# Eight PSUM banks shared out anew in a fused attention and mixer kernel: from 2 + 2 + 4 to 3 + 2 + 3

## The chip, the cores and the metric

The kernel runs on one core of one Trainium2 chip. The metric is the time of one execution on the device in microseconds (us), and the figure that counts is the median of several runs.

## What is computed

The inputs are q, k and v (8 batches, 8 heads, 576 tokens, 64 numbers per head) and seven weight matrices. Cut to what matters:

```python
k_p = k.reshape(B, H, 72, 8, D).mean(axis=3)      # keys and values pooled by eights
v_p = v.reshape(B, H, 72, 8, D).mean(axis=3)
attn = softmax(q @ k_p.T / sqrt(D)) @ v_p          # x: (8, 576, 512)
theta = x @ w_theta
y = w_tok_r @ (x * cos(theta)) + w_tok_i @ (x * sin(theta))
u = x + y
x = u + relu(u @ w_ch)
h = relu(x.T @ w_tok1) @ w_tok2                    # over tokens
u = x + h.T
out = u + relu(u @ w_ch1) @ w_ch2
```

## The kernel before

The work runs in three stretches. The **attention stage** goes up to about 545 us of the span: a prologue computes attention for batch 0 and converts the weights, and then a loop over the eight batches does the token products of batch b while it computes, in between, the attention, the angles and the factors of batch b + 1. After it come the channel product and the token mixer (to about 775 us) and the large channel mixer (to the end).

Every matrix product and every transpose writes into one of eight PSUM banks of 512 numbers per partition. A bank is taken by name. Three kinds of names exist, and each kind is handed out in rotation by its own counter (line 129):

- **m** (line 137): the token products. `mix_part` (line 770) takes one for each group of 27 matrix products (line 786). The bank is free again when VectorE has added it to the tile R (line 789).
- **t** (line 140): theta, in `emit_theta` (line 676). Free when ScalarE has read it (line 705) and VectorE has subtracted it (line 718).
- **x** (line 143): all the rest of the attention stage. `emit_sc` (line 538) takes two for each pair of heads, for scores of chunks 0 to 1 and 2 to 4; VectorE frees them by a maximum and a subtraction (lines 552 and 553). `emit_pt` (line 579) takes two for each transpose of the softmax; ScalarE copies them (604, 608) and VectorE takes the rest (605, 610). `emit_av` (line 616) takes one for each product with the values; ScalarE copies it twice (645, 646) and VectorE frees it (650). `emit_z` (line 725) takes one for the transposes of R; VectorE frees it (736, 745). In batch 0 the copies are those of lines 601 and 631. `pool_k`, `pool_v` and `pool_vl` take some x banks in the prologue.

```python
    def bank(kind, n):
        i = bank_i.get(kind, 0)
        bank_i[kind] = i + 1
        nm = f"{kind}{i % n}"
        need(nm)
```

The token products of a batch are eight groups of 27. `interleave` (line 793) puts the steps of the next batch's attention between them at moments that the table `P` (line 20) lists. The program is then put in its final order by a scheduler, engine by engine, which goes by its own estimate of when a bank or a tile is free. So the order of the instructions is fixed before the kernel runs, and an engine that comes to an instruction whose bank is still in use waits there, with all that stands behind it in its queue. The softmax of a pair of heads runs over three engines: subtract on VectorE (553), exponent on ScalarE (558), sum and reciprocal on VectorE (564, 565, 568), scaling on GpSimd (569, 574). The tile R gets a copy of its tail by line 536 before theta of the last token chunk can begin.

In the two later stretches all eight banks are taken in one fixed rotation by `bank_any` (line 148).

Of the kernel before, what the change touches and what calls it, by code (L numbers as in the profile page):

```python
# [64 lines left out]
def tile_attn_moe(  # L65
# [43 lines left out]
    def need(*tags):  # L109
        while any(t in d[3] for d in dq for t in tags):  # L110
            run_one()
# [17 lines left out]
# [5 lines that stand above are left out]
        last_bank[0] = nm  # L134
        return pp.tile([128, 512], F32, tag=nm, name=nm)

    def bank_m():
        return bank("m", 2)

    def bank_t():  # L140
        return bank("t", 2)

    def bank_x():
        return bank("x", 4)

    allseq = [0]

    def bank_any():
        i = allseq[0] % 8
        allseq[0] += 1  # L150
        nm = ("m0", "t0", "x0", "x1", "m1", "t1", "x2", "x3")[i]
        need(nm)
        return pp.tile([128, 512], F32, tag=nm, name=nm)

# [316 lines left out]
    def pool_k(b, g):  # L471
        t, m = kn_t[b], pool_t[0]
        ps = bank_x()
        for i in range(2):
            ds = slice((2 * g + i) * 128, (2 * g + i + 1) * 128)
            o = ps[:, i * 80:i * 80 + 80]
            for c in range(4):
                mm(o[:, 8 + 16 * c:24 + 16 * c], t[:, c, ds], m[:, 0:16], True, True)
            for c0 in (0, 72):
                mm(o[:, c0:c0 + 8], t[0:64, 4, ds], m[0:64, 0:8], True, True)  # L480
        v = ps[:, 0:160].rearrange("p (g k) -> p g k", g=2)
        nc.vector.tensor_copy(out=bdk[0:64, 2 * g:2 * g + 2, 0:72], in_=v[0:64, :, 0:72])
        nc.scalar.copy(out=bdk[64:128, 2 * g:2 * g + 2, 72:144], in_=v[64:128, :, 8:80])

    def pool_v(b):
        t, m = vn_t[b], pool_t[0]
        ps = bank_x()
        for c in range(4):
            mm(ps, m[:, 64 - 16 * c:192 - 16 * c], t[:, c], c == 0, c == 3)
        v = ps.rearrange("p (j e d) -> p j e d", j=4, e=2)  # L490
        for e in range(2):
            pr = slice(64 * e, 64 * e + 64)
            if b == 0:
                (nc.vector.tensor_copy, nc.scalar.copy)[e](out=vb0[pr, :, pr], in_=v[pr, :, e])
            else:
                nc.scalar.copy(out=vbh[pr, :, pr], in_=v[pr, :, e])
        if b > 0:
            def fin():
                for e in range(2):
                    pr = slice(64 * e, 64 * e + 64)  # L500
                    nc.vector.tensor_sub(
                        out=vlo["b"][pr, :, pr], in0=v[pr, :, e], in1=vbh[pr, :, pr].bitcast(F32)
                    )

            later(1.0, fin, last_bank[0], "vbl")

    def pool_vl(b):
        t, m = vn_t[b], pool_t[0]
        ps = bank_x()
        mm(ps, m[0:64, 192:320], t[0:64, 4], True, True)  # L510
        v = ps.rearrange("p (h d) -> p h d", h=8)

        def masked(o, pr):
            nc.vector.tensor_tensor(
                out=o[pr].rearrange("p a e d -> p (a e) d"), in0=v[pr],
                in1=mask[pr].unsqueeze(2).to_broadcast([64, 8, 64]), op=ALU.mult,
            )

        lo, up = slice(0, 64), slice(64, 128)
        if b == 0:  # L520
            masked(vl0, lo)
            return
        tm = st("kr", [128, 4, 2, 64], F32, "vlt")
        vll = vlo["l"]
        masked(tm, lo)
        masked(vlh, up)
        nc.scalar.copy(out=vlh[lo], in_=tm[lo])
        nc.gpsimd.tensor_sub(out=vll[lo], in0=tm[lo], in1=vlh[lo].bitcast(F32))
# [241 lines left out]
    def mix_part(b, half, jj, th, part, hold):  # L770
        j = 2 * half + jj
        t0, n = TH[th]
        ts = slice(t0, t0 + n)
        if part == 0:
            hold["ps"] = bank_m()
        o = hold["ps"][:, 0:n]
        need(f"Z{half}", f"zt{b % 2}")
        z, zt = z_t[b, half], zt_t[b]
        for i in range(part * 3, part * 3 + 3):
            (a, w), s = HL3[i // 9], i % 9  # L780
            cq_upto(9 + s + 9 * th)
            if s < 8:
                lhsT = z[:, a, s // 4, s % 4, jj * 128:(jj + 1) * 128]
            else:
                lhsT = zt[:, a, j * 128:(j + 1) * 128]
            mm(o, lhsT, wtk[s][:, w, ts], i == 0, i == 26)
        if part == 8:
            R = r_t[b]
            nc.vector.tensor_add(out=R[:, j, ts], in0=o, in1=R[:, j, ts])  # L789
            if th == 1:  # L790
                nc.sync.dma_start(out=scr_u[b][:, j, :], in_=R[:, j, 0:T])
# [75 lines left out]
    def emit_ch(b, j, th):  # L867
        t0, n = TH[th]
        ts = slice(t0, t0 + n)
        h = uh_t[b]  # L870
        o = bank_any()[:, 0:n]
        i = 0
        for a, w in HL3:
            for k in range(4):
                mm(o, wch[k][:, w, j * 128:(j + 1) * 128], h[a][:, k, ts], i == 0, i == 11)
                i += 1
        u = u_t[b][:, j, ts]
        nc.vector.scalar_tensor_tensor(out=u, in0=o, scalar=0.0, in1=u, op0=ALU.max, op1=ALU.add)
        gate[0] = u[0:1, 0:1]
        if j == 3 and th == 1:  # L880
            dup_tail(u_t[b], nc.scalar.copy)

    def emit_tr(b, c):
        u = u_t[b]
        if c == 0:
            x2_t[b] = (st("Z0", [128, 2, 4, 512], F32R, "x2"), st("zt0", [128, 512], F32R, "x2t"))
        x2, x2t = x2_t[b]
        ps = bank_any()
        for d in range(4):
            src = u[:, d, c * 128:(c + 1) * 128]  # L890
            tp(ps[:, d * 128:(d + 1) * 128], src)
        if c < 4:
            nc.scalar.copy(out=x2[:, 0, c, :], in_=ps)
            nc.vector.tensor_sub(out=x2[:, 1, c, :], in0=ps, in1=x2[:, 0, c, :].bitcast(F32))
        else:
            nc.scalar.copy(out=x2t, in_=ps)
            lo = x2t[64:128]
            nc.vector.tensor_sub(out=lo, in0=ps[64:128], in1=lo.bitcast(F32))

    def emit_tok1(b, f):  # L900
        x2, x2t = x2_t[b]
        w1 = A2["tok1"]
        if f == 0:
            h1_t[b] = (st("tmp0", [128, 2, 512], F32R, "h1a"), st("tmp1", [128, 2, 512], F32R, "h1b"))
        fs = slice(f * 128, (f + 1) * 128)
        ps = bank_any()
        seq = [(w1[:, w, s, fs], x2[:, a, s, :]) for a, w in HL3 for s in range(4)]
        seq += [(w1[:, 0, 4, fs], x2t), (w1[:, 1, 4, fs], x2t)]
        for i, (l, r) in enumerate(seq):
            mm(ps, l, r, i == 0, i == len(seq) - 1)  # L910
        h = h1_t[b][f]
        nc.scalar.activation(out=h[:, 0], in_=ps, func=ACTF.Relu)
        nc.vector.scalar_tensor_tensor(
            out=h[:, 1], in0=ps, scalar=0.0, in1=h[:, 0].bitcast(F32), op0=ALU.max, op1=ALU.subtract
        )
# [726 lines left out]
```

## Time and profile before

| | |
|---|---|
| Median of 3 runs | 1333.22 us (1333.06 to 1338.38) |
| The profiled execution | 1337.11 us |
| Its span, first to last instruction | 1335.3 us |
| TensorE busy with matrix products | 1277.9 us, 96% of the span |
| VectorE busy | 976.6 us, 73% |
| ScalarE busy | 637.1 us, 48% |
| GpSimd busy | 315.5 us, 24% |
| Granted TensorE clock, mean | 0.993 of full speed |

PE stands for TensorE, PEld for its weight loads, DVE for VectorE, ACT for ScalarE, POOL for GpSimd. In the timeline views a row gives the start, the time to the end of the last of the merged instructions, the engine and line, what is written from what (buffer numbers left out), and how many instructions are merged; in square brackets stands the idle time of the engine just before, and what ended it.

### The profile page before, as it was taken

The page shows a single profiled execution, that of the slowest core. Times are in us where ns is not written, and L with a number is a line of the kernel's source. Part 1 is how long each engine was busy: PE and PEld are TensorE (multiplying, and loading weights), DVE is VectorE, ACT ScalarE, POOL GpSimd, SP SyncE. Part 2 cuts the span into 40 slices and gives each one's busy share as a digit, 9 for nine tenths or more (in the row PEclk, how much of TensorE's full clock was granted, in tenths as well). Part 3 has the DMA queues.
Part 4 walks back from the last instruction along what each step waited for, and adds up shares of the span by engine and source line. Part 5 has one row for each costly group of instructions (what it writes and reads, how often), then busy time and mean ns, then how long its engine had stood idle before and what let it go on. Part 6 is the DMA issues. An engine that isn't in the chain of part 4 may idle for free.

```text
span 1335.3 us, 22342 instructions
## 1 busy us (share of the span) xinstructions
PE 1277.9 (96%) x8214; PEld 1216.5 (91%) x8216; DVE 976.6 (73%) x1749; ACT 637.1 (48%) x1190; POOL 315.5 (24%) x340
## 2 busy tenths in 40 slices
PE   6899999999999999999999999999999999999998
PEld 4588999999999998998889988888999999999998
DVE  7987667584958696566676768688665489987893
ACT  4765454555564564233333246466454354444442
POOL 4553324232433533111110001111100013133112
PEclk9999999999999999999999999999999999999999
DMA  9423122221322023445567367767544986556521
GB/s 330 145 81 118 58 97 81 85 91 60 108 64 69 28 89 115 145 162 211 196 237 261 128 206 256 237 202 244 202 155 166 335 318 216 163 187 208 185 94 69
DMA packets 119613, 213.70 MB, mean 160 GB/s; under 512 B 11152, under 2 KB 65936, under 8 KB 119504
## 3 DMA queue, kind: packets, MB, share of 16 engines
q1 hardware_dynamic: 119504, 212.29, 46.9%
q8 instruction: 64, 1.05, 0.3%
q14 instruction: 45, 0.37, 0.1%
HBM read 133.60 MB, written 78.64 MB: 159 GB/s over the span
## 4 chain that ended last, share of the span: by engine, by line
PE 55%; DVE 21%; issue 11%; DMA 8%; POOL 2%; ACT 2%; SPq 0%; DVEq 0%; POOLq 0%; ACTq 0%
PE x L159 20%; PE m L159 18%; PE t L159 15%; DMA scr_g<-g 2%; DVE sm L564 2%; PE x L173 2%; DVE e L553 2%; DVE mx L552 2%; DMA raw_n<-scr_x 1%; DVE tmp L736 1%; DMA scr_w<-wo 1%; DVE sm L565 1%; POOL wo L1024 1%; DMA ws<-w_ch 1%; DVE R L789 1%
## 5 line engine op out<-in xcount | busy, mean ns | idle before, releaser
L159 PE MATMUL m<-wtk,Z 128*128 128x256 f32 (+1 forms) x1536 | 247.1, 300 | 7.4 <-DVE R L789 7.1
L159 PEld LDWEIGHTS m<-wtk,Z 128*128 128x128 f32 x1536 | 218.0, 190 | 10.7 <-DVE R L789 7.7
L751 POOL TENSOR_TENSOR Z<-tmp,Z 128x1024 fp32r<-128x1024 f32 x31 | 74.7, 2411 | 110.9 <-ACT Z L750 110.9
L1012 POOL TENSOR_TENSOR wsum<-wm 128x128 f32<-128x128 f32 (+1 forms) x18 | 10.8, 602 | 298.8 <-DVE wm L1002 281.7
L159 PE MATMUL t<-wth,Xh 128*128 128x256 f32 (+1 forms) x504 | 76.5, 293 | 0.5 <-DVE Xh L536 0.2
L1364 POOL TENSOR_TENSOR o<-o,u 128x384 f32<-128x384 f32 x12 | 16.2, 1374 | 244.5 <-DVE u L1352 156.3
L159 PEld LDWEIGHTS t<-wth,Xh 128*128 128x128 f32 x504 | 67.0, 188 | 4.5 <-DVE Xh L536 1.8
L718 DVE SCALAR_TENSOR_TENSOR tmp<-tmp,t 128x512 f32<-128x512 f32 x40 | 27.3, 684 | 53.9 <-ACT tmp L705 53.9
L159 PE MATMUL x<-ope_Xl,wa 128*128 128x384 f32 x336 | 65.4, 336 | 0.1
L159 PE MATMUL m<-ope_Z,wa 128*128 128x384 f32 x300 | 63.7, 337 | 1.3 <-ACT p L1264 0.6
L159 PE MATMUL x<-ope_R,wa 128*128 128x384 f32 x312 | 62.4, 340 | 0.7 <-DVE p L1281 0.7
L736 DVE TENSOR_TENSOR tmp<-x,tmp 128x1024 f32<-128x1024 f32 x32 | 39.1, 1221 | 31.1 <-ACT tmp L712 16.0
L159 PE MATMUL x<-ope_Z,wa 128*128 128x384 f32 x276 | 56.1, 339 | 4.4 <-ACT p L1277 2.5
L159 PEld LDWEIGHTS x<-ope_Xl,wa 128*128 128x128 f32 x336 | 58.8, 188 | 0.4 <-DVE ope_Xl L1126 0.4
L159 PE MATMUL x<-bdk,q 128*128 128x144 f32 x320 | 47.9, 303 | 11.5 <-DVE bdk L1423 7.0
L159 PEld LDWEIGHTS x<-ope_R,wa 128*128 128x128 f32 x312 | 54.6, 188 | 2.6 <-DVE p L1281 1.8
L159 PEld LDWEIGHTS x<-bdk,q 128*128 128x128 f32 x320 | 44.4, 203 | 13.6 <-issue 10.8
L159 PE MATMUL m<-wtk,zt 128*128 128x256 f32 (+1 forms) x192 | 56.8, 296 | 0.0
L159 PE MATMUL x<-ope_Xh,wa 128*128 128x384 f32 x264 | 54.9, 340 | 1.9 <-DVE p L1281 0.8
L159 PEld LDWEIGHTS m<-ope_Z,wa 128*128 128x128 f32 x300 | 52.9, 188 | 2.2 <-ACT p L1264 0.9
L159 PEld LDWEIGHTS x<-ope_Z,wa 128*128 128x128 f32 x276 | 48.2, 188 | 6.7 <-ACT p L1277 3.5
L705 ACT ACTIVATE tmp<-t,magic 128x512 f32<-128x512 f32 x40 | 27.3, 684 | 55.6 <-PE t L159 42.8
(412 smaller groups left out, 3521.6 us busy)
## 6 DMA issues: line engine op xcount, KB each, us to landing
wa<-scr_w SPq DMA_DIRECT2D x42, 512.0 KB, 5.5
scr_g<-g SPq DMA_DIRECT2D x108, 192.0 KB, 2.4
scr_w<-wo SPq DMA_DIRECT2D x42, 256.0 KB, 2.7
scr_u<-R SPq DMA_DIRECT2D x32, 288.0 KB, 2.1
u<-scr_u SPq DMA_DIRECT2D x32, 288.0 KB, 4.1
scr_w<-wo SPq DMA_DIRECT2D x18, 512.0 KB, 3.1
scr_x<-u SPq DMA_DIRECT2D x32, 288.0 KB, 2.8
raw_n<-scr_x SPq DMA_DIRECT2D x24, 384.0 KB, 3.9
```

The source lines that it names most:

```text
L159: nc.tensor.matmul(out=o, lhsT=l, rhs=r, start=start, stop=stop, skip_group_check=skip)
L173: nc.tensor.transpose(o, i, ident)
L552: nc.vector.tensor_reduce(out=mx[:, c0:c1, :], in_=v, axis=AX.X, op=ALU.max)
L553: nc.vector.tensor_tensor(out=e[:, c0:c1, 2 * p:2 * p + 2, :], in0=v, in1=mx[:, c0:c1, :].unsqueeze(3).to_broadcast([128, n, 2, 72]), op=A ...
L564: nc.vector.tensor_reduce(out=sm, in_=ep, axis=AX.X, op=ALU.add)
L565: nc.vector.tensor_scalar(out=sm, in0=sm, scalar1=1e-9, scalar2=8.0, op0=ALU.add, op1=ALU.mult)
L705: nc.scalar.activation(out=t, in_=pt, func=ACTF.Identity, bias=magic[:, 0:1])
L718: nc.vector.scalar_tensor_tensor(out=t, in0=t, scalar=MAGIC, in1=pt, op0=ALU.subtract, op1=ALU.subtract)
L736: nc.vector.tensor_tensor(out=tmp, in0=px.unsqueeze(1).to_broadcast([128, 2, 512]), in1=tmp, op=ALU.mult)
L751: later(1.0 if lo is nc.vector else 0.0, lambda: lo.tensor_sub(out=zl, in0=zv, in1=zh.bitcast(F32)), tg, zg)
L789: nc.vector.tensor_add(out=R[:, j, ts], in0=o, in1=R[:, j, ts])
L1364: nc.gpsimd.tensor_tensor(out=u22[d].t, in0=u22[d].t, in1=u2[d].t, op=ALU.add)
```

## The change

The tags of the rotation change: m gets a third bank, x gives up its fourth. The last place of the rotation in the later stretches takes the new name. Theta keeps two.

```diff
     def bank_m():
-        return bank("m", 2)
+        return bank("m", 3)
...
     def bank_x():
-        return bank("x", 4)
+        return bank("x", 3)
...
     def bank_any():
         i = allseq[0] % 8
         allseq[0] += 1
-        nm = ("m0", "t0", "x0", "x1", "m1", "t1", "x2", "x3")[i]
+        nm = ("m0", "t0", "x0", "x1", "m1", "t1", "x2", "m2")[i]
```

The scheduler then sets another order on all engines. Three places follow, each as a piece of the difference.

TensorE, in the middle of the token products of batch 2 (tile m_2223 is a group of token products, the x tiles are the scores of the third and fourth pair of heads of batch 3):

```order
 L159 MATMUL m_2223<-wtk_517,Z_1897 128x320
 L159 MATMUL x_2231<-bdk,q_1516 128x144 x2
+L159 MATMUL x_2253<-bdk,q_1516 128x144 x2
 L159 MATMUL x_2238<-bdk,q_1516 128x144 x3
-L159 MATMUL x_2253<-bdk,q_1516 128x144 x2
-L159 MATMUL x_2258<-bdk,q_1516 128x144 x3
 L159 MATMUL m_2223<-wtk_552,Z_1897 128x320
 L159 MATMUL m_2223<-wtk_559,Z_1897 128x320
```

Before, the four score tiles stood together, each in a bank of its own. Now three stand together, and the fourth, which has to take the bank of x_2231, stands ten token products later:

```order
 L159 MATMUL m_2223<-wtk_517,Z_1897 128x320
 L159 MATMUL m_2223<-wtk_552,Z_1897 128x320
+L159 MATMUL x_2258<-bdk,q_1516 128x144 x3
 L159 MATMUL m_2223<-wtk_559,Z_1897 128x320
 L159 MATMUL m_2223<-wtk_594,zt_1879 128x320
```

The same move stands in batches 1 to 5.

TensorE, in the token products of batch 0 (the tiles x_967 to x_982 are the transposed softmax of the first two pairs of heads of batch 1, m_917 and m_946 two groups of token products):

```order
 L159 MATMUL m_917<-wtk_559,Z_531 128x256
 L159 MATMUL m_917<-wtk_594,zt_523 128x256
-L173 MATMUL x_967<-con,e 128x128 x2
-L173 MATMUL x_971<-con,e 128x128 x3
-L173 MATMUL x_978<-con,e 128x128 x2
-L173 MATMUL x_982<-con,e 128x128 x3
 L159 MATMUL m_946<-wtk_473,Z_531 128x320
 L159 MATMUL m_946<-wtk_481,Z_531 128x320
```

The four transposes stood ahead of the group m_946. Now they stand between its products, the first of them behind 15.

VectorE, in the prologue (R_346 is the tile R of batch 0, its line 536 the copy of the tail; the other rows convert weights):

```order
 L261 SCALAR_TENSOR_TENSOR early_103<-early_w_107,early_103 128x288
 L267 SCALAR_TENSOR_TENSOR early_103<-early_w_106,early_103 128x288
-L536 COPY R_346<-R_346 128x4x64
 L267 SCALAR_TENSOR_TENSOR early_103<-early_w_107,early_103 128x288
+L631 COPY R_346<-x_454 128x256
 L255 TENSOR_SCALAR early_104<-early_104 128x288 x2
 L261 SCALAR_TENSOR_TENSOR early_104<-early_w_108,early_104 128x288
+L295 TENSOR_TENSOR wtk_594<-early_103,wtk_594 128x288
 L261 SCALAR_TENSOR_TENSOR early_104<-early,early_104 128x288
-L295 TENSOR_TENSOR wtk_594<-early_103,wtk_594 128x288
+L536 COPY R_346<-R_346 128x4x64
 L267 SCALAR_TENSOR_TENSOR early_104<-early_w_108,early_104 128x288
```

The copies of the attention products of batch 0 (lines 601 and 631) and the tail copy stand about six VectorE instructions later than before.

## Rows read from the trace of the kernel before

**Rows 1.** The page: span, and busy time of TensorE and its weight loads.

```profile
span 1335.3 us, 22342 instructions
PE 1277.9 (96%) x8214; PEld 1216.5 (91%) x8216; DVE 976.6 (73%) x1749; ACT 637.1 (48%) x1190; POOL 315.5 (24%) x340
```

**Rows 2.** Waits of TensorE, 145 to 447 us (total us, times, longest).

```profile
PE m L159 <- DVE R L789: 4.2, 5, 0.9
PE x L159 <- DVE t L610: 1.5, 5, 0.3
PE x L159 <- DVE pt L605: 0.9, 5, 0.2
```

**Rows 3.** Windows: length; busy us of PE, PEld, DVE, ACT, POOL; clock; DMA.

```profile
99.00:104.00 5.00, 3.29 (x20) 2.24 (x19) 4.94 (x15) 2.89 (x6) 3.49 (x7) 0.87 0.38 131
104.00:106.00 2.00, 2.00 (x8) 2.00 (x9) 2.00 (x4) 0.11 (x1) 0.95 (x3) 0.50 0.00 0
205.00:245.00 40.00, 38.75 (x303) 37.83 (x301) 32.09 (x66) 21.39 (x45) 14.82 (x17) 1.00 0.28 97
508.00:513.00 5.00, 4.59 (x25) 4.39 (x25) 4.97 (x11) 1.05 (x3) 3.37 (x3) 0.66 0.00 0
```

**Rows 4.** Timeline of TensorE, 216 to 247 us (token products of batch 2).

```profile
217.17 2.61 PE L159 MATMUL x<-bdk,q 128*128 128x144 f32 x20
219.53 0.55 PE L159 MATMUL m<-wtk,Z 128*128 128x320 f32 x2
...
220.06 1.33 PE L159 MATMUL m<-wtk,Z 128*128 128x320 f32 x8
...
221.38 1.33 PE L159 MATMUL m<-wtk,Z 128*128 128x320 f32 x8
...
226.84 1.44 PE L159 MATMUL m<-wtk,Z 128*128 128x320 f32 x8 [0.80 <-DVE R L789]
...
228.70 0.71 PE L173 MATMUL x<-con,e 128*128 128x128 f32 x5
...
232.71 0.71 PE L173 MATMUL x<-con,pl 128*128 128x128 f32 x5
...
234.79 0.39 PE L159 MATMUL x<-t,vlh 128*128 128x256 f32 x1 [0.30 <-DVE t L610]
...
242.77 0.40 PE L159 MATMUL m<-wtk,Z 128*128 128x256 f32 x2
```

**Rows 5.** Timeline of VectorE in the same stretch.

```profile
218.72 2.13 DVE L565 TENSOR_SCALAR sm<-sm 128x10 f32<-128x10 f32 x1
...
221.26 0.45 DVE L553 TENSOR_TENSOR e<-x,mx 128x288 f32<-128x288 f32 x1
...
226.30 0.48 DVE L789 TENSOR_TENSOR R<-m,R 128x320 f32<-128x320 f32 x1
...
234.31 0.83 DVE L610 TENSOR_TENSOR t<-x,t 64x256 fp32r<-64x256 f32 x2
```

**Rows 6.** Timeline of GpSimd in the same stretch.

```profile
218.45 2.38 POOL L751 TENSOR_TENSOR Z<-tmp,Z 128x1024 fp32r<-128x1024 f32 x1 [2.48 <-ACT Z L750]
```

**Rows 7.** Timeline of VectorE, prologue and start of batch 0.

```profile
53.84 0.52 DVE L536 COPY R<-R 128x256 f32<-128x256 f32 x1
...
58.31 0.45 DVE L267 SCALAR_TENSOR_TENSOR early<-early_w,early 128x288 uint32<-128x288 uint32 x1
...
83.55 0.30 DVE L482 COPY bdk<-x 64x144 f32<-64x144 f32 x1 [3.11 <-PE x L159]
```

**Rows 8.** Timeline of TensorE: prologue, batch 0 and batch 7.

```profile
54.41 7.56 PE L159 MATMUL t<-wt,R 128*128 128x512 f32 x18 [3.10 <-DVE R L536]
...
103.74 2.50 PE L159 MATMUL m<-wtk,Z 128*128 128x320 f32 x8
...
507.19 0.47 PE L159 MATMUL m<-wtk,Z 128*128 128x256 f32 x2 [1.52 <-DVE R L789]
...
513.10 1.15 PE L159 MATMUL m<-wtk,Z 128*128 128x320 f32 x6 [0.52 <-DVE R L789]
```

## The prediction

> **What bounds the kernel now.** I read the page first: TensorE is busy for 1277.9 us of a span of 1335.3 us [rows 1]. No instruction of TensorE is added or removed, so the change can act only through the 57 us in which it idles, and through the clock. The page lists all stretches of the kernel; only the attention stage, up to about 545 us, hands out m and x banks by kind. Behind it the eight banks go round in the same fixed order with one name exchanged, so I cost that part at nothing.
>
> Next I read what TensorE waits for in the five batches that look alike, 145 to 447 us [rows 2]. Three waits come once a batch: 4.2 us in five times for the add of a token group into R (line 789), 1.5 us for the small half of the transposed tile t (line 610), and 0.9 us for line 605. The first is a shortage of m banks, the other two are a VectorE that is late. The sum is 6.6 us, or 1.3 us a batch. The window of one batch says the same: TensorE is busy for 38.75 of 40 us, at the full clock [rows 3].
>
> Then I read one batch in the timelines. The m wait is the idle 0.80 us ahead of the group that starts at 226.84 [rows 4]. It ends with the add at 226.30 [rows 5], and that add is late because VectorE has the scores to reduce and, among them, a tiny line 565 that took 2.13 us [rows 5] while GpSimd's line 751 ran [rows 6]. So here VectorE sets the pace, and TensorE runs into it wherever it needs a bank back.
>
> **The change, part by part.**
>
> *The m wait, batches 1 to 5.* With a third m bank the group at 226.84 takes a bank that was freed long before. The 0.80 us go: 5 x 0.80 = 4.0 us, if TensorE comes there no later than before.
>
> *The fourth score tile, batches 1 to 5.* It does come later. Before, the four score tiles of the third and fourth pair went out together as 20 matrix products from 217.17, and the next group began at 219.53: 0.118 us each [rows 4]. Now the fourth tile, x_2258, has to take the bank of x_2231, and stands behind the other three (14 products, 1.65 us) and ten token products, which take 1.32 us for nine (220.06 to 221.38) and so 1.47 us. TensorE reaches x_2258 at 217.17 + 1.65 + 1.47 = 220.29. The bank is free when VectorE's line 553 ends, at 221.26 + 0.45 = 221.71 [rows 5]. VectorE's order is unchanged here, and line 565 and GpSimd hold it as before. So there is a **new wait of 1.4 us**, with the token products, the third m bank among them, queued behind it. It is the price of the x bank, and it takes the place of the wait of 0.80 us: TensorE comes to the m group 0.6 us later than now. Lower bound 0 (line 565 is not held, VectorE is 2 us earlier); upper bound 1.4 plus the 0.3 us by which TensorE could come earlier still.
>
> *The wait for tile t.* Eight us further on TensorE waited 0.30 us for line 610 [rows 4] and about 0.2 us for line 605 [rows 2]. VectorE's time there does not depend on these 0.6 us, since its queue has no gap, so the waits shrink by what TensorE is late: -0.5 us. The batch stands at +0.1 us.
>
> *Transposes and value products on three banks.* From 228.70 to 242.77, 14.1 us, 18 x tiles pass [rows 4]. On three banks they need 18 x hold / 3, where hold is the time from the first product to the last read. The t tiles, two of the 18, show a hold: 232.71 [rows 4] to 234.31 + 0.83 = 235.14 [rows 5], 2.4 us, for two that started together. 18 x 2.4 / 3 = 14.4 us, 0.3 us over the 14.1. These were late tiles, and the new order puts token products into the gaps, so I take +0.2 us. Lower bound 0; upper bound with a hold of 2.7 us, 16.2 us, +2.1. Sum of a batch: +0.3 us, five batches +1.5 us.
>
> *Batch 0.* Between 99 and 104 us TensorE is busy for 3.29 of 5 us [rows 3]: it waits for the softmax of batch 1 at the four transposes that now stand inside the group m_946. These 1.7 us can go. At their end the granted clock was at its lower level, 0.50 of full speed from 104 to 106 [rows 3], and eight token products took 2.50 us [rows 8] against 1.33 at the full clock [rows 4]: another 1.2 us. Together -2.9 us. Against it: the tail copy of R in the prologue stands behind what ran from 54.3 to 58.31 [rows 7], so theta of batch 0 begins 4.0 us later. TensorE already idled 3.10 us for it [rows 8]. VectorE's later work is the same in sum, and it idles 3.11 us ahead of 83.55 [rows 7], so most of the 4.0 is taken up there: +0.9 us (0 to 4). The chain of transposes and value products of batch 1 follows here without room: 14 tiles at 2.4 us on three banks instead of four is 14 x 2.4 x (1/3 - 1/4) = 2.8 us, and the token products that were saved up cover about half: +1.2 us (0 to 2.8). Batch 0: -2.9 + 0.9 + 1.2 = -0.8 us.
>
> *Batches 6 and 7.* In batch 6 the waits belong to VectorE, which then converts late weights: 0. In batch 7 the m wait of 0.52 us at 513.10 goes [rows 8]: -0.5 us. The 1.52 us at 507.19 are for Z, a product of VectorE and ScalarE, and stay.
>
> *The clock.* At 507 us two waits within a microsecond of work are followed by a lower clock, 0.66 in the mean from 508 to 513 [rows 3]; in the alike batches, with 0.80 and 0.30 us, it stays at 1.00. I take it that one wait of 1.4 us leaves the clock alone: 0. The Trainium skill, page "TensorE: Matmul & The Clock Gate", section "A second HAM failure mode: psum-queue depth-cycling", says the opposite of cycling through PSUM banks: short idles between groups can be frequent enough to throw the clock back and forth. By that rule the sum would be higher by the price of the second rival below.
>
> *Sum:* -0.8 + 1.5 + 0 - 0.5 = +0.2 us. Against the profiled execution (1337.11 us; its span is 1335.3) that is 1337.3 us. That execution lies 3.9 us above the median of the runs, and +0.2 us on the median of 1333.22 is **1333.4 us**.
>
> **The rivals.**
>
> *Faster: the m waits go and nothing comes.* This needs x_2258 to find its bank free: VectorE must end line 553 about 1.4 us earlier against TensorE, as it would if the new order of the transposes changes when GpSimd's line 751 holds line 565. For it: GpSimd's order does change, once, at the factors of batch 1. Against: in the five batches the orders of VectorE and GpSimd at that point are those of before. Price: 5 x 0.80 + 2.9 + 0.5 = 7.4 us, and up to 10 with the waits for t: about 1325 us.
>
> *Slower: three banks become the chain that sets the pace.* It decides from a hold of 2.35 us on (14.1 x 3 / 18). At 2.7 us each of six batches is 2.1 us longer and the new order cannot fill it; with the 0.1 us from the waits and no gain in batch 0: +13 - 0.5 = about 1345 us; at 2.5 us about 1338. For it: the one hold that I read is 2.4 us. Against: a TensorE that comes later finds VectorE and ScalarE less behind, and holds shrink.
>
> *Slower: the clock falls once a batch.* Each fall costs what it did in batch 0, 1.2 us for eight products, or 2 us if it lasts through 508 to 513 (0.34 of 5 us): 5 x 1.2 to 5 x 2, 1339 to 1343 us. For it: a single longer wait than now. Against: the clock of 1.00 in all like batches.
>
> *The prologue is not caught up:* +4 us, 1337 us.
>
> **How the numbers follow.** Forecast 0.58, faster rival 0.14, three banks 0.13, clock 0.08, prologue 0.07. About 0.5%, 6.7 us, is what a measurement can tell from no change; the three runs alone lie 5.3 us apart. Of the faster rival 0.09 lies below 1326.5 us; of the slower ones 0.09 of the chain and 0.03 of the clock lie above 1339.9; the rest is the same: 0.09, 0.79, 0.12. The range goes from 1327, which leaves out the far part of the faster rival, to 1340, which takes in the prologue, the chain at 2.5 us and the cheaper clock; about 0.2 is left out.
>
> **What would show it.** In the waits of TensorE, line 789 falls from five times to none in batches 1 to 5, and a wait of x for line 553 of over 1 us appears once in each of them; with no such wait, that step is wrong. The idle time between 99 and 104 us falls, and theta of batch 0 starts near 58 us instead of 54.4. TensorE's busy time and instruction count stay. A clock under 1.00 in batches 1 to 5, or a period of a batch that is longer than now by over 1 us, would make the forecast wrong on the slow side; a period shorter by over 0.5 us on the fast side.

## The result, and the profile after

The changed kernel takes 1349.8 us (1345.5 to 1354.1, 4 runs) against 1333.1 us (1332.7 to 1338.4, 4 runs) of the kernel before: a ratio of 1.0113, 95% interval 1.0092 to 1.0134. It is **slower by 1.1%**; the two medians lie 16.7 us apart. The forecast was 1333.4 us, 1327 to 1340.

The page of the changed kernel, its span and TensorE (to be held against [rows 1]):

```profile
span 1348.2 us, 22344 instructions
PE 1282.8 (95%) x8214; PEld 1217.9 (90%) x8216; DVE 981.6 (73%) x1749; ACT 639.3 (47%) x1190; POOL 319.3 (24%) x340
```

The work is the same, the idle time is not: 65.4 us of it where there were 57.4. TensorE's busy time is 4.9 us more as well: 5.0 more up to the last angle tile of batch 0, where the clock is lower, 2.8 more in the five like batches, where it is 1.00 in both, and 2.9 less in the rest. So not all of it is the clock: the records of products overlap (20 of them from 217.17 last 2.61 us, but the next group begins at 219.53 [rows 4]), and a short wait can lie within busy time.

Where the time goes is best read by lining up the same weight load in both traces. Four of them are used here: the first 512-wide angle product of batch 0 (at 54.4 us before), the last angle tile of batch 0 (t_721, 74.6 us), the first angle tile of the loop over batch 1 (t_1394, 144.0 us) and the second of the loop over batch 6 (t_4843, 448.0 us; the first gives the same losses to 0.02 us a batch). The changed kernel is late there by 7.0, 10.9, 10.5 and 16.8 us. So the **prologue**, here up to t_721, **costs 10.9 us**, batch 0 gives 0.4 back, and **batches 1 to 5 cost 1.26 us each**, (16.8 - 10.5) / 5. Behind 560 us nothing is lost. (The spans differ by 12.9 us alone: the profiled execution of before lies 3.9 us over its median, and it is slow in the later stretches, where the changed kernel's trace makes up 3.9 us on it from 520 us on, and those of twelve of the thirteen experiments 0.4 to 7.5 us.)

**The five like batches.** TensorE's waits of the changed kernel, 145 to 462 us (total us, times, longest), against [rows 2]:

```profile
PE x L159 <- DVE e L553: 6.8, 5, 1.4
PE t L159 <- DVE Xh L536: 2.4, 5, 0.5
PE x L159 <- DVE pt L605: 1.2, 5, 0.3
```

The m wait and the wait for line 610 are gone. The wait for line 553 is there, 1.36 us five times, as forecast. A wait of 0.5 us for the tail copy of Xh (line 536) is five times there where it came once before. In the timelines of TensorE, VectorE and GpSimd, batch 2 of the changed kernel, against [rows 4 to 6]:

```profile
229.09 1.88 PE L159 MATMUL x<-bdk,q 128*128 128x144 f32 x14
...
233.80 0.97 PE L159 MATMUL x<-bdk,q 128*128 128x144 f32 x6 [1.37 <-DVE e L553]
...
250.91 0.77 PE L173 MATMUL x<-con,e 128*128 128x128 f32 x5
...
254.15 0.41 PE L159 MATMUL x<-pt,vbh 128*128 128x320 f32 x1 [0.26 <-DVE pt L605]
...
258.11 1.20 PE L159 MATMUL t<-wth,Xh 128*128 128x512 f32 x4 [0.47 <-DVE Xh L536]
```

```profile
230.80 2.00 DVE L565 TENSOR_SCALAR sm<-sm 128x10 f32<-128x10 f32 x1
...
233.20 0.45 DVE L553 TENSOR_TENSOR e<-x,mx 128x288 f32<-128x288 f32 x1
...
252.48 1.21 DVE L410 TENSOR_REDUCE sums<-vr 128x128 f32<-128x1024 f32 x1
253.61 0.48 DVE L605 TENSOR_TENSOR pt<-x,pt 128x320 fp32r<-128x320 f32 x1
...
256.93 1.12 DVE L536 CAST Xh<-Xh 128x256 fp32r<-128x256 f32 x1
```

```profile
230.38 2.39 POOL L751 TENSOR_TENSOR Z<-tmp,Z 128x1024 fp32r<-128x1024 f32 x1 [2.65 <-ACT Z L750]
```

Line 565 is held until GpSimd's line 751 ends (232.8), line 553 ends at 233.65, and the fourth score tile starts at 233.80. Twenty us further on, a value product waits for the bank that line 605 frees at 254.09, and theta for the tail copy that ends at 258.05. Both are the chain of transposes and value products on three banks, and here the batch loses its time: TensorE is 11.8 us late at the first angle tile of this batch's loop, 12.1 us at the value product before the one at 254.15, 12.8 us at that one, and 13.0 us at the next theta. That product now has to take the bank of the second transpose of 250.91, which is read until 254.09; with four names it took the bank of the first, which was free earlier.

The windows of one batch and of five, against [rows 3]:

```profile
217.00:258.00 41.00, 39.02 (x301) 37.71 (x299) 32.48 (x66) 21.69 (x45) 14.62 (x17) 1.00 0.28 95
160.00:460.00 300.00, 289.47 (x2192) 280.36 (x2191) 211.20 (x411) 161.26 (x302) 100.74 (x98) 1.00 0.24 78
```

The clock is at its upper level throughout; the waits of 1.4, 0.3 and 0.5 us in a batch are not followed by a lower one.

**The prologue.** TensorE's timeline, first before, then after:

```profile
19.98 2.35 PE L159 MATMUL x<-nat_Xl,pool 128*128 128x512 f32 x4 [0.26 <-PE x L159]
...
31.74 0.77 PE L173 MATMUL x<-con,pl 128*128 128x128 f32 x5 [1.43 <-POOL pl L574]
...
62.96 3.72 PE L159 MATMUL t<-wt,R 128*128 128x256 f32 x16 [0.56 <-DVE tmp L718]
```

```profile
21.48 2.05 PE L159 MATMUL x<-nat_Xl,pool 128*128 128x512 f32 x2 [1.41 <-issue]
...
35.30 1.33 PE L173 MATMUL x<-con,pl 128*128 128x128 f32 x5 [2.88 <-POOL pl L574]
...
61.43 7.56 PE L159 MATMUL t<-wt,R 128*128 128x512 f32 x18 [3.21 <-DVE R L536]
...
71.34 5.41 PE L159 MATMUL t<-wt,R 128*128 128x256 f32 x16 [1.92 <-DVE tmp L718]
...
81.79 0.50 PE L159 MATMUL m<-wtk,Z 128*128 128x256 f32 x2 [1.14 <-ACT Z L750]
...
85.53 5.41 PE L159 MATMUL t<-wt,R 128*128 128x256 f32 x16
```

Five things differ, in order of time. The pooled values (x_245) wait 1.41 us where they waited 0.26. The row names no releaser; by the bank names it is the bank: the ninth x tile takes the bank of the sixth, which VectorE frees late, where with four names it took that of the fifth. The transposes of the small tile t wait 2.88 us for GpSimd's line 574 instead of 1.43. Theta comes at 61.43 instead of 54.41. The next angle tile waits 1.92 us for line 718 instead of 0.56, and its 16 products take 5.41 us instead of 3.72, at a lower clock. And the first two token products wait 1.14 us for Z: in TensorE's new order they stand earlier, ahead of a tile of 24 short products and of the last angle tile:

```
-L159 MATMUL t_695<-wt_290,R_346 128x256 x8
+L159 MATMUL t_695<-wt_290,R_346 128x256 x7
+L159 MATMUL m_684<-wtk_473,Z_531 128x256
+L159 MATMUL m_684<-wtk_481,Z_531 128x256
+L159 MATMUL t_695<-wt_290,R_346 128x256
...
-L159 MATMUL t_721<-wt_290,R_346 128x256
-L159 MATMUL m_684<-wtk_473,Z_531 128x256
-L159 MATMUL m_684<-wtk_481,Z_531 128x256
```

Theta waits for VectorE's tail copy (line 536). Up to theta VectorE has carried out 118 instructions instead of 112, 3.0 us more work, and has idled 4.0 us longer, 3.1 us of it for TensorE's transposes. VectorE's timeline, before, then after:

```profile
32.22 0.42 DVE L601 COPY t<-x 64x256 f32<-64x256 f32 x1 [0.26 <-PE x L173]
```

```profile
36.02 0.42 DVE L601 COPY t<-x 64x256 f32<-64x256 f32 x1 [2.54 <-PE x L173]
...
39.73 0.42 DVE L601 COPY pt<-x 128x256 f32<-128x256 f32 x1 [0.79 <-PE x L173]
...
61.09 0.28 DVE L536 COPY R<-R 128x256 f32<-128x256 f32 x1
```

VectorE's idle time behind theta, which was to take the delay up [rows 7], comes again 7.9 us later, now for transposes that stand behind the last angle tile in TensorE's queue (the changed kernel):

```profile
91.48 1.23 DVE L736 TENSOR_TENSOR tmp<-x,tmp 128x1024 f32<-128x1024 f32 x1 [3.67 <-PE x L173]
```

### The profile page after: what moved, and what is told of

Read it like the earlier page. It is cut to its first block, busy times and chain, and to the rows that moved or that the text cites. A ratio compares the mean times of both kernels' runs of the same rounds, so it can differ in the third digit from the quotient of the medians.

```text
span 1348.2 us, 22344 instructions
## 1 busy us (share of the span) xinstructions
PE 1282.8 (95%) x8214; PEld 1217.9 (90%) x8216; DVE 981.6 (73%) x1749; ACT 639.3 (47%) x1190; POOL 319.3 (24%) x340
## 4 chain that ended last, share of the span: by engine, by line
PE 60%; DVE 15%; issue 11%; DMA 9%; POOL 3%; ACT 2%; SPq 0%; DVEq 0%; POOLq 0%; ACTq 0%
PE m L159 26%; PE x L159 16%; PE t L159 15%; PE x L173 2%; DMA scr_w<-wo 2%; DMA raw_n<-scr_x 1%; DMA scr_g<-g 1%; DVE sm L564 1%; POOL wo L1024 1%; DVE sm L565 1%; DVE tmp L736 1%; DVE e L553 1%; DMA early<-w_tok 1%; DVE early L261 1%; DMA ws<-w_ch 1%
## 5 line engine op out<-in xcount | busy, mean ns | idle before, releaser
L159 PE MATMUL m<-wtk,Z 128*128 128x256 f32 (+1 forms) x1536 | 251.6, 300 | 5.8 <-ACT Z L750 4.1
L159 PE MATMUL m<-ope_Z,wa 128*128 128x384 f32 x336 | 71.8, 338 | 2.0 <-DVE p L1281 1.3
L159 PEld LDWEIGHTS m<-ope_Z,wa 128*128 128x128 f32 x336 | 59.1, 188 | 4.0 <-DVE p L1281 2.2
L159 PE MATMUL m<-ope_R,wa 128*128 128x384 f32 x270 | 57.2, 340 | 2.1 <-ACT p L1264 1.4
L159 PE MATMUL t<-ope_Z,wa 128*128 128x384 f32 x252 | 53.6, 335 | 0.0
L569 POOL TENSOR_TENSOR e<-e,sm 128x720 f32<-128x720 f32 x32 | 45.4, 1419 | 33.5 <-DVE sm L568 26.0
L159 PE MATMUL x<-ope_Z,wa 128*128 128x384 f32 x240 | 48.5, 338 | 3.2 <-ACT p L1277 2.8
L159 PEld LDWEIGHTS m<-ope_R,wa 128*128 128x128 f32 x270 | 47.4, 188 | 4.3 <-ACT p L1264 2.3
L558 ACT ACTIVATE e<-e 128x720 f32<-128x720 f32 x32 | 25.8, 805 | 50.3 <-DVE e L553 50.1
L159 PE MATMUL m<-ope_Xh,wa 128*128 128x384 f32 x222 | 48.3, 338 | 0.8 <-DVE p L1281 0.8
```

Of the source, the lines that this page charges most:

```text
L159: nc.tensor.matmul(out=o, lhsT=l, rhs=r, start=start, stop=stop, skip_group_check=skip)
L558: nc.scalar.activation(out=ep, in_=ep, func=ACTF.Exp, scale=1.0 / 64.0)
L569: nc.gpsimd.tensor_tensor(out=ep, in0=ep, in1=sm.unsqueeze(3).to_broadcast([128, 5, 2, 72]), op=ALU.mult)
```

## The experiments

Where an experiment changes which x banks are used, `bank_x` is told who asks and goes round four names, leaving one out by a rule (NAMES stands for a tuple of names, RULE for a function of the name n; e8, with six names, takes their number in place of 4):

```diff
-    def bank_x():
-        return bank("x", 3)
+    def bank_x(use="", b=0):
+        nm = last_bank[0] = x_name(bank_i, NAMES, RULE); need(nm); return pp.tile([128, 512], F32, tag=nm, name=nm)
...
+def x_name(bank_i, order, left_out):
+    i = bank_i.get("x", 0)
+    while left_out(order[i % 4]):
+        i += 1
+    bank_i["x"] = i + 1
+    return order[i % 4]
```

The table gives for each run the ratio to the kernel before with its 95% interval, the start of the first 512-wide angle product (54.41 us before, 61.43 after), how late t_1394 is against the trace of before, and the loss of a batch, (lateness of t_4843 - lateness of t_1394) / 5. Each of these is read from one trace; e2, e8, e12 and e13, whose loop has the banks of before, give -0.10 to +0.03 us a batch, which is how far that column can be trusted.

| run | ratio | angle product, us | t_1394 late, us | per batch, us |
|---|---|---|---|---|
| the change | 1.0113 (1.0092 to 1.0134) | 61.43 | 10.5 | +1.26 |
| e1 | 1.0059 (1.0036 to 1.0081) | 54.86 | 0.9 | +1.12 |
| e2 | 1.0129 (1.0088 to 1.0169) | 60.41 | 16.0 | -0.10 |
| e3 | 1.0012 (0.9996 to 1.0028) | 55.61 | 2.2 | +0.16 |
| e4 | 1.0061 (1.0043 to 1.0079) | 55.31 | 3.6 | +0.94 |
| e5 | 1.0144 (1.0113 to 1.0175) | 62.03 | 14.7 | +1.18 |
| e6 | 1.0031 (1.0012 to 1.0050) | 57.77 | 8.0 | -0.62 |
| e7 | 0.9952 (0.9932 to 0.9972) | 60.16 | 6.0 | -1.96 |
| e8 | 1.0005 (0.9984 to 1.0027) | 56.66 | 1.1 | -0.07 |
| e9 | 1.0071 (1.0043 to 1.0099) | 55.52 | 3.1 | +1.17 |
| e10 | 0.9948 (0.9931 to 0.9965) | 55.51 | 2.1 | -1.97 |
| e11 | 0.9992 (0.9971 to 1.0013) | 54.41 | 2.2 | -0.61 |
| e12 | 1.0076 (1.0048 to 1.0103) | 57.32 | 10.8 | +0.03 |
| e13 | 1.0056 (1.0022 to 1.0091) | 58.00 | 11.1 | +0.02 |

**Prologue or loop: e1 and e2.**

```diff
NAMES = ("x0", "x1", "x2", "m2"); RULE: n == "m2" and b > 0      # e1, on the changed kernel
NAMES = ("x0", "x1", "x2", "x3"); RULE: n == "x3" and b == 0     # e2, on the kernel before
```

> The changed kernel, but all attention work of batch 0 (the prologue) may take m2 as a fourth x bank, since token products take none before 75 us; batches 1 to 7 keep 3 + 2 + 3. Theory A (the shortage of x banks in the prologue makes most of the loss, the loop about 1.2 us a batch): the prologue's order of instructions is again that of the kernel before, theta of batch 0 starts at 54.4 us +- 0.5 as before instead of 61.4, the first token products near 75 instead of 82, and 9 to 11 us come back: 1337 to 1341 us. Theory B (the third m bank makes the loss, wherever it is): nothing comes back, 1347 to 1352. Theory C (the clock falls in the batches): nothing comes back that does not come with a higher clock in batches 1 to 5, which is 1.00 already.

> The kernel before (2 + 2 + 4), but the attention work of batch 0 leaves x3 out and goes on three x banks; batches 1 to 7 keep four. Theory A: the same loss as in the changed kernel, without a third m bank: theta of batch 0 starts at 61.4 us +- 1, the first token products at about 82, and 9 to 12 us are lost in all: 1342 to 1346 us. Theory B: within 2 us of the kernel before, 1331 to 1336.

e1 measured 1339.9 us. Its prologue is again that of before:

```profile
54.86 7.56 PE L159 MATMUL t<-wt,R 128*128 128x512 f32 x18 [3.10 <-DVE R L536]
```

By the traces 9.6 us come back up to t_1394, by the ratios some 7 us, and the 1.1 us of a batch stay. e2 measured 1349.9 us (1339.7 to 1352.1): with two m banks and four x banks in the loop, three x banks in batch 0 alone cost as much as the whole change, and the batches then cost nothing. Up to beyond the last angle tile of batch 0 its order is that of the changed kernel, instruction for instruction on TensorE, VectorE, ScalarE and GpSimd. It lost more than expected, 16.0 us at t_1394, and its clock was lower, 0.64 in the mean from 80 to 100 us against 0.91 in the changed kernel. That it comes out level with the whole change is therefore chance. Theory A holds, and B, the third m bank as the cause, falls.

**Inside a batch: e3, e4 and e9.**

```diff
RULE: n == "x3" and (b > 0 and use == "sc")      # e3, on the kernel before
RULE: n == "x3" and (b > 0 and use != "sc")      # e4, on the kernel before
RULE: n == "x3" and b > 0                        # e9, on the kernel before: e1 without the third m bank
```

> The kernel before, but the scores of batches 1 to 7 leave x3 out; transposes, value products and the prologue keep four x banks, m two. Theory A: TensorE waits about 1.4 us for line 553 once in each of batches 1 to 5; the waits for m (line 789, 0.8 us) and for tile t (0.3 us) shrink by what TensorE is late, so that a batch is longer by only 0.1 to 0.4 us: 1333 to 1336. Rival (the wait for the scores is the whole loss of a batch, and nothing takes it back): 1.2 to 1.4 us a batch, 1340 to 1343.

> The kernel before, but the transposes and value products of batches 1 to 7 leave x3 out; scores and the prologue keep four x banks, m two. Theory A: the chain of transposes and value products paces TensorE at its end, and the copies of the tail (line 536) come late for theta: 0.8 to 1.2 us a batch, seven batches, 1338 to 1342, with the m wait of 0.8 us still there. Rival (token products fill the gaps): 0.2 us a batch, 1333 to 1335.

> As e1 (four x banks for the work of batch 0, three for batches 1 to 7), but with only two m banks: in the loop one of the eight banks is not used. It differs from e1 by the third m bank alone. Theory A (the third m bank is worth next to nothing, since the wait for the fourth score tile and the late end of the value products put TensorE behind the add of line 789): batches 1 to 5 lose 1.1 to 1.3 us each against the kernel before, as in e1 (1.2), and the time is within 3 us of e1's 1339.9, 1337 to 1342. Rival (the third m bank saves the 0.8 us a batch that it was to save): 1.9 to 2.1 us a batch, 1343 to 1346.

TensorE's waits over the like batches, e3, then e4, then e9:

```profile
PE x L159 <- DVE e L553: 6.8, 5, 1.4
PE x L159 <- DVE t L610: 1.1, 5, 0.2
PE t L159 <- DVE Xh L536: 0.2, 1, 0.2
```

```profile
PE m L159 <- DVE R L789: 4.7, 5, 1.3
PE x L159 <- DVE pt L605: 3.3, 9, 0.5
PE t L159 <- DVE Xh L536: 2.4, 5, 0.5
```

```profile
PE x L159 <- DVE e L553: 6.8, 5, 1.4
PE t L159 <- DVE Xh L536: 2.4, 5, 0.5
PE x L159 <- DVE pt L605: 1.3, 5, 0.3
```

In e3 the wait of 1.36 us is there, the m wait is gone although there are only two m banks, and a batch is longer by 0.16 us, little more than the column's scatter: the exchange of one wait for the other that the prediction worked out. In e4 the m wait stays and the batch loses 0.94 us, with the wait for the tail copy: this is where the loss of a batch lies. (In its batch 2 TensorE is 4.2 to 4.3 us late at the first angle tile and at the value product before the last two, and 5.0 and 5.1 at these, the same step as in the changed kernel; the pooled values and transposes of R, which e4 also puts on three banks, lose nothing there.) e9 has the same three waits as the changed kernel to 0.1 us, and 1.17 us a batch against 1.12 in e1: **the third m bank saves nothing in these batches**, since TensorE comes to the m group late enough without it.

**What makes VectorE late: e6, e7, e10 and e11.** Line 565 goes, and its factor moves into the copies of the value products (e6 in the changed kernel, e7 in the kernel before, with lines up to three off; e10 and e11 in batches 1 to 7 alone, on the kernels of before and of e1):

```diff
-        nc.vector.tensor_scalar(
-            out=sm, in0=sm, scalar1=1e-9, scalar2=8.0, op0=ALU.add, op1=ALU.mult
-        )
...
-        nc.scalar.copy(out=h[:, j, ts], in_=o)
+        nc.scalar.mul(h[:, j, ts], o, 0.125)
...
-            nc.vector.tensor_sub(out=l[:, j, ts], in0=o, in1=h[:, j, ts].bitcast(F32))
+            nc.vector.scalar_tensor_tensor(out=l[:, j, ts], in0=o, scalar=0.125, in1=h[:, j, ts].bitcast(F32), op0=ALU.mult, op1=ALU.subtract)
```

> The changed kernel without line 565: the factor 8 leaves the sum of the softmax (1e-9 is lost against a sum of at least 1 in float32), and the copies of the value products (lines 631, 645, 646, 650) multiply by 0.125. Theory A (line 565, held 2.1 us while GpSimd's line 751 runs, makes line 553 late, and with it the fourth score tile): the waits for line 553 in batches 1 to 5 fall from 1.4 us to under 0.3, and no other VectorE line takes over the 2.1 us. The gain is 0.3 to 1 us a batch, since only part of that wait lasts to the end of a batch: 1343 to 1348. Rival (another small line, 568, is held in its place): the waits stay at 1.0 to 1.4 and the time within 2 us of 1349.8.

> The kernel before (2 + 2 + 4) without line 565, edited in the same way. Theory A: line 565 is also what makes the add of line 789 late, so the m wait of 0.8 us and the waits for t (0.3) and pt (0.2) shrink: 0.5 to 1.3 us a batch, six batches, 1323 to 1329. That would say that VectorE's lateness, and not the number of banks, was the cause of the waits for m. Rival: line 568 is held in its place, within 2 us of the kernel before.

> The kernel before (2 + 2 + 4); line 565 and the factor 0.125 are moved as in e7, but for batches 1 to 7 alone, so that the prologue keeps its order. Theory A (e7 gained 1.9 us in each like batch and lost 5.7 us in its prologue only because the scheduler set another order there, with no bank taken away): the prologue is that of the kernel before to 0.5 us, the batches gain 1.9 us each, and the time is 10 to 13 us under the kernel before: 1319 to 1324. Rival (the prologue of e7 was late for the removed line itself): 1325 to 1329 as e7.

> The edit of e10 on the kernel of e1 (three m banks, three x banks in the loop, four in the prologue). Theory A: the wait for line 553 goes, and what is left against e10 is the chain of transposes and value products on three banks, 1.0 to 1.3 us a batch: 6 to 9 us over e10, 1327 to 1332. Rival (with VectorE on time three banks are enough, and the third m bank pays): within 2 us of e10.

In e6, 1339.5 us, the waits for line 553 are gone and a batch is 1.9 us shorter than in the changed kernel, twice what was expected. In e7, 1327.9 us, all that TensorE still waits for between 145 and 460 us is

```profile
PE t L159 <- DVE Xh L536: 0.2, 1, 0.2
```

and a batch is 1.96 us shorter than before, though the named waits [rows 2] made only 1.3: of the 9.8 us of five batches 6.6 are idle time and 3.2 are busy time, at the same clock of 1.00. So nearly the whole hold of 2.0 to 2.1 us reached TensorE, whichever bank it showed up at. No other small line was held in its place: the reciprocal (line 568) takes 196 to 210 ns in the like batches of before, the change, e2, e5 and e6. e7's prologue came 5.8 us late, with the orders of all engines changed there though no bank was. e10 keeps the prologue's order and is **the fastest kernel here by its median, 1325.7 us, 0.5% under the kernel before** (e7's interval overlaps with its); it missed its expected 1319 to 1324: its trace is 2.1 us late at t_1394, of which more below, and loses 1.5 us in batch 7. e11 is 1331.3 us: with VectorE on time the three x banks still cost 1.36 us a batch against e10, and the third m bank does not make up for it.

**The prologue from inside: e5, e8, e12 and e13.**

```diff
-        emit_pt(0, 4)
         emit_pt(0, 0)
+        emit_pt(0, 4)                               # e5, on the changed kernel
...
NAMES = ("x0", "x1", "x2", "x3", "m0", "m1"); RULE: n[0] == "m" and (b > 0 or use == "z")    # e8, on the kernel before
RULE: n == "x3" and b == 0 and use in ("sc", "pool")     # e12, on the kernel before
RULE: n == "x3" and b == 0 and use in ("pt", "av")       # e13, on the kernel before
```

> The changed kernel with one edit in the prologue: the transposes of the first pair of heads (line 1432) are emitted ahead of those of the small tile t (line 1431). Theory A' (on three banks the two t tiles, x_301 and x_308, hold two of three banks from about 29 us, while GpSimd's line 574 makes their input, and the transposes of the pairs wait behind them in TensorE's queue): the wait of 2.9 us for line 574 shrinks by 1 to 2.5 us, theta of batch 0 starts 1.5 to 4 us earlier than 61.4, and the time is 1345 to 1348. Rival (VectorE's order of copies and weight conversions sets theta, whatever the order of the transposes): theta within 1 us of 61.4, 1348 to 1351.

> The kernel before, but in the prologue the x tiles may take m0 and m1 also, six banks; everything behind it as before. Theory A (in the prologue the number of x banks sets when TensorE's queue can go on: three banks cost 6 to 7 us up to theta): with six, theta of batch 0 starts 0.5 to 3 us earlier than 54.4, and the time is 1328 to 1331. Rival (four banks are enough, VectorE's conversions set theta): theta within 0.5 us of 54.4, 1330 to 1334.

> The kernel before, but in the prologue only the scores and the pooled values of batch 0 leave x3 out; its transposes, value products and angles keep four x banks. Theory S (the loss up to theta starts at the scores: in the changed kernel the pooled values, x_245, wait 1.4 us for a score bank, and the softmax of the last pair is 2.4 us late): theta of batch 0 starts 3 us or more after 54.4. Theory T (it is made by the transposes, of which three banks hold fewer ahead): theta within 2 us of 54.4 (which the unchanged prologue also varies by, 0 to 2 us), and 1331 to 1336 us.

> The kernel before, but in the prologue only the transposes and value products of batch 0 leave x3 out; scores, pooled values and angles keep four. Theory T: theta of batch 0 starts 4 us or more after 54.4, the first token products 6 to 11 us later, 1339 to 1346 us. Theory S: theta within 2 us of 54.4, 1331 to 1336 us.

e5: theory A' falls. The wait for line 574 is still 2.8 us, theta at 62.03 and the time, 1352.9 us, above both ranges; the order of these transposes is not the cause. e8: two more banks gain nothing; theta is 2.3 us later, and the scheduler had set yet another order. With e7 this says that the order counts, and not the number of banks alone. No run has the new order with four banks, or the old one with three, so what the order costs in the prologue and what the missing bank costs is not told apart. e12 and e13: neither use of the bank makes the loss up to theta alone, and theories S and T both miss their bounds for theta. Theta is 2.9 us late without the fourth bank for scores, 3.6 us without it for transposes, 6.5 us together, against 6.0 in e2. Only in e12, as in the changed kernel and e2, do the pooled values wait 1.4 to 1.5 us for a score bank.

Behind theta both lose 7 to 8 us more up to t_1394. TensorE's timeline and a window of e13, then TensorE's timeline of e2:

```profile
76.94 0.50 PE L159 MATMUL m<-wtk,Z 128*128 128x256 f32 x2 [2.44 <-ACT Z L750]
...
77.97 5.44 PE L159 MATMUL x<-pool,nat_Xl 128*128 128x16 f32 x24
...
83.34 5.84 PE L159 MATMUL t<-wt,R 128*128 128x256 f32 x16
```

```profile
78.00:86.00 8.00, 8.00 (x31) 7.40 (x30) 4.43 (x6) 3.80 (x7) 2.57 (x3) 0.50 0.27 98
```

```profile
70.32 3.72 PE L159 MATMUL t<-wt,R 128*128 128x256 f32 x16 [1.92 <-DVE tmp L718]
...
80.76 0.50 PE L159 MATMUL m<-wtk,Z 128*128 128x256 f32 x2 [2.82 <-ACT Z L750]
```

In e2, e12 and e13, as in the changed kernel, the two token products stand that early and wait for Z. After that idle time (2.4 to 2.8 us in these three) the granted clock stays at 0.50 to 0.52 for 8 us, and 24 products that take 3.03 us at the full clock (the changed kernel, 82.56) take 5.44. In the changed kernel the wait is 1.14 us and the clock falls for less. Its wait is shorter since it had lost the time before: the 16 products ahead took 5.41 us at a lower clock, in e2, with the same order, 3.72 at the full one. That is 1.7 us more of work and 1.7 us less of waiting; ScalarE ends Z just before the products start in both, so Z sets the time here, and that fall of the clock cost nothing up to this point.

## Why the prediction was wrong

- **The prologue: the step that failed.** It read: "VectorE's later work is the same in sum, and it idles 3.11 us ahead of 83.55 [rows 7], so most of the 4.0 is taken up there: +0.9 us (0 to 4)". Measured: 10.9 us. Two errors lie in it. The 4.0 us came from VectorE's order alone, and of the 7.0 us up to theta that order makes 3.0; the other 4.0 are VectorE's longer idle time, 3.1 of it for transposes. TensorE's order in the prologue, where x_245 waits for its bank and the transposes stand behind the 2.88 us wait for line 574, was not walked. And the idle time that was to cover the delay ended with products of TensorE that stand in its queue behind the last angle tiles: it lies behind the late work on the same chain and moves with it. A further 3.9 us come behind theta, of which the rows show 3.7: line 718 (+1.4), the wait for Z (+1.1) and a lower clock (+1.7 in 16 products, 5.41 against 3.72; e2 shows that this and the wait for Z stand in for each other), less the 0.5 us of a second wait for line 718 that went. The rival "the prologue is not caught up" had half of the mechanism, at 4 us and a chance of 0.07.
- **The m wait goes: right, and it pays nothing.** Five waits of line 789 became none; but so they did in e3 with two m banks.
- **The fourth score tile: right.** 1.4 us forecast, 1.36 measured, with the cause named, line 565 held by GpSimd's line 751. The Trainium skill, page "SBUF — State Buffer", section "Who interferes with whom", says that a tensor_scalar on VectorE may take a port pair that it shares with GpSimd, and that whichever engine comes second waits for the whole instruction of the first. The trace agrees: 0.16 us in the median, 2.0 us where it meets line 751, and the two end together.
- **Waits for t: right.** The waits for lines 610 and 605 at that place both went; the wait for line 605 that is listed now stands at another product, the one at 254.15. Scores on three banks as a whole cost 0.16 us a batch in e3; the prediction had +0.1.
- **Transposes and value products on three banks: mis-sized.** The term was +0.2 us a batch (0 to 2.1); e4 measured 0.94. By the mean there was room: worked out tile by tile from the trace of before, the 18 holds run from 1.4 to 3.5 us with a mean of 2.24, which is 18 x 2.24 / 3 = 13.4 us on three banks in a stretch of 14.1. What the sum lacked is that one long hold stops the queue: the tile whose line 605 stands behind a reduction of 1.21 us (2.96 us in the changed kernel) now blocks the last but one value product, and the tail copy, at the end of that chain, is what theta waits for. Five batches cost 6.3 us instead of 1.5. The sign that the prediction named for this side, a batch longer by over 1 us, came.
- **Batch 0: right in sign, too large.** Its own part was -1.7 us and measured -0.4 (10.9 to 10.5 us late). The low clock went, 1.00 from 110 to 125 us, where the same work now stands; the idle 1.7 us came back as waits of 1.1 us for line 605 and 0.7 us for line 574 at 116 and 120 us.
- **Batches 6 and 7:** 0 and -0.5 us forecast, +0.5 and -0.5 measured (16.8, 17.3, 16.8 us late). The second is luck: the waits for m are gone there, but behind them TensorE waits longer for Z (the row of 507.19 names line 789 for the 1.52 us that the prediction gave to Z), and what pays for it is a clock of 1.00 where it had been 0.66 [rows 3]. TensorE and a window of the changed kernel:

```profile
524.97 0.97 PE L159 MATMUL m<-wtk,Z 128*128 128x256 f32 x6 [2.92 <-ACT Z L750]
...
529.06 0.97 PE L159 MATMUL m<-wtk,Z 128*128 128x256 f32 x6 [1.76 <-POOL Z L751]
```

```profile
521.00:526.00 5.00, 2.08 (x17) 1.88 (x16) 5.00 (x18) 2.08 (x4) 1.67 (x2) 1.00 0.29 79
526.00:530.00 4.00, 2.23 (x20) 2.04 (x19) 3.94 (x7) 0.73 (x2) 4.00 (x3) 1.00 0.00 0
```

- **The later stretches** cost nothing, as said.
- **The clock in the batches: right**, 1.00 from 160 to 460 us. The rule of the Trainium skill on cycling through PSUM banks (page "TensorE: Matmul & The Clock Gate", section "A second HAM failure mode: psum-queue depth-cycling") would have it go back and forth there; no run here shows that in the loop. The clock did matter in the prologue, where the prediction had not looked. (Its price of a longer fall, 2 us, should have been 0.34 x 5 = 1.7.)
- **The sum.** 10.0 us too little for the prologue, 4.8 for the five like batches, 1.3 for batch 0 and 0.5 for batch 6 make the 16.6 us between 0.2 and 16.8. That the one trace's 16.8 us fits the 16.7 us between the medians so well is luck: the runs of the changed kernel alone lie 8.6 us apart.

## What to carry to other kernels

Idle time covers a delay only if it does not wait for the delayed work itself: follow what ends it before counting on it, and walk every engine's order, not only the one whose copies moved. A wait for a buffer names the place where a late engine is felt, not its cause; taking a bank from the scores moved the wait from line 789 to line 553, while taking away the tiny instruction that held VectorE was worth nearly 2 us a batch under either sharing. A mean hold that fits says little where one tile is held longer than the rest. And where a scheduler sets the order, a count that serves several stages changes the order in all of them: change it per stage, as e1 did, which kept the prologue's old order.

## What the runs showed of the hardware

A VectorE instruction of 0.16 us on 10 numbers a partition was held 2.0 to 2.1 us, once a batch, and without it a batch was 1.9 to 2.0 us shorter. The length of one idle time does not tell whether TensorE's clock falls: in e13 it stood at 0.50 for 8 us behind an idle time of 2.44 us, while the changed kernel kept 1.00 through 1.4 us in the loop and through 2.92 and 1.76 us in batch 7; and in the trace of before it was 0.57 from 75 to 79 us, though TensorE had not idled for more than 0.56 us at a time since 54.4. And the seven kernels whose prologue has the order of before (before itself, e1, e3, e4, e9, e10 and e11) start the angle product between 54.41 and 55.61 us: a difference of 1 us in one trace of the prologue says nothing.
